# End of a top-k attention ahead of a routed expert layer: three scales and the first block of a weight split made ahead of a branch

## The chip, the cores and the metric

One core of a Trainium2 chip runs the whole kernel. The metric is the time of one execution on the device in microseconds (us). PE is TensorE, ACT is ScalarE, DVE is VectorE, POOL is GpSimd; SP issues the transfers named here.

## The reference

Attention with a top-k mask feeds a routed expert layer, whose output feeds a second layer with a rational function between its two products. Cut to what matters:

```
scores = q @ k.T / 8                       # 4 x 8 heads, 576 x 576, depth 64
mask   = scores >= 32nd largest of the row
attn   = softmax(where(mask, scores, -1e9))
x      = attn @ v                          # as (2304, 512)
logits = x @ w_gate                        # (2304, 8)
# all 2304 * 8 entries in falling order: token -> expert,
# unless the token is taken or the expert has 288 tokens
for e in range(8):
    m = assigned == e
    x2[m] = relu(x[m] @ w1[e]) @ w2[e]     # 512 x 1024, 1024 x 512
h = x2 @ w_in                              # 512 x 2048
g = (a0 + a1 h + a2 h^2 + a3 h^3) / (1 + |b0||h| + |b1|h^2 + 1e-6)
out = g @ w_out                            # 2048 x 512
```

## The kernel before

Products of the layers behind the routing run in fp16 as three products of halves: each fp32 operand is multiplied by a power of two and split into a rounded fp16 "high" and a remainder "low" (lines L1954, L1955 and L1956 are the three products). The power of two comes from a sum of squares (weights) or a maximum (x); four small DVE instructions on a 128 x 1 column turn that number into the scale and its inverse (`power_steps`, L293 to L298).

The program goes through these stages.

1. Attention, 72 units of two heads each; it ends in `finish_attention`. There a planner, the object `last` of class `Flow`, takes tasks (engine, cost, function, what they wait for, rank) and writes them out in the order in which they could start by its costs, lower ranks first; tasks of rank 1000 and above only fill. Beside the last units it places the router's logits: PE turns x (L1200), DVE copies (`xt`, L1206), PE multiplies (L1210), DVE copies (`lt`, L1221), PE turns back (L1224), DVE copies (`lg`, L1249). ACT sums x's squares there (L1228), and, as filling, the squares of the first expert's w1 and w2 (`conv_stats`, the `wsum` rows of L306).
2. A branch, `tc.If` at L1338: a value that DVE wrote (`odd`, L1305) is loaded by every engine, and where it isn't zero the attention is computed again. It is zero here, so every engine jumps over that code. Behind it the first instruction of most engines waits for all five engines' sequencers.
3. Routing: seven phases of four search steps, each a chain DVE (compare, L1552), PE (count, L1560), DVE (L1624), PE (L1628), DVE (L1636). At a phase's end PE counts with L1718. In the gaps a second planner, `flow`, places other work: the split of w_in and w_out, and the first expert's weights (`add_first`: highs on ACT, L1430; remainders on PE, L1494 twice and L1495 once for 256 columns; a copy on ACT, L1498).
4. A second branch at L1904, jumped over too. Behind it POOL gathers the first expert's rows of x (L1931, `xe`), PE turns them (L1966), ACT and DVE split them (`xT`, L1944 and L1945), and PE multiplies with w1 and w2 (`pe`). ACT and DVE take those products out (`hT`, `x`) and, between them, split what is left of w_in and w_out.
5. The second layer in pairs of product groups (`ph` from w_in, `po` from w_out), expert after expert, until the end.

The split of a weight goes in blocks of four pieces of 128 x 512 (`add_block`, called with the block's scales `s` and `inv`): w_in has four blocks (0 to 3), w_out four. Each piece arrives by a transfer on SP into a slot with its upper halves in place. ACT then makes a sign (L383), a magnitude (L384) and a shifted word (L385), or for later pieces in a ring buffer two steps (L373, L377); DVE adds the lower bits (`mantissa`, L408) and the sign (L412, or L395 for the ring), in wholes of 512 or in halves of 256 columns; ACT squares with a sum (L306, output `junk`, sum `nq`); DVE sums four sums (L427) and takes the four power steps; ACT makes the four highs (L436); DVE makes the four lows (L440), and a low frees its slot, on which SP fetches a further piece (L340). The fetches that become free behind the first branch are the eight at 463.88. A later block's highs wait for the block before to have its lows, since they write over each other's slots.

Before the first branch, the first six pieces have their three ACT steps done, and the first three of them (`EV = 3`) mantissa and sign. Everything else of `add_block` stands behind the branch, as do the first expert's two weight scales (`scale_steps`: a product with ones, L1414, a sum, L1419, four power steps) and x's scale (L1511, then `everywhere_steps`: maximum, L1391, PE turns it, L1384, maximum, L1393, PE spreads it, L1388, copy, L1395, then four power steps to `s_x` and `i_x`). x's scale is needed by `xT` and by the settling of w_in's four scales to a common one (`settle_in`, L1445 to L1447). `settle_out` does the same for w_out from `s_out` (the `ev_m` of 128 x 16).

## Time and profile before

| what | us |
|---|---|
| three runs | 1224.65, 1225.04, 1227.86 |
| median | 1225.04 |
| the profiled execution's own time | 1223.68 |
| its span, first to last instruction | 1222.0 |
| attention's last output x (DVE, L905) | 446.86 |
| the last logits' copy (DVE, L1249) | 459.45 |
| first work behind the first branch | 463.08 to 463.95 |
| the last of the routing's slots (DVE, L1798) | 560.30 |
| expert 0's products with w1, w2 begin | 574.91 |
| the first `ph` group's square sums on PE (L2086) | 620.60 |

Granted TensorE clock over the span: 0.921 of 2.4 GHz. Busy over the span: PE 91%, DVE 86%, ACT 83%, POOL 31%. These shares are means over stages with different limits: from 446 to 463 and from 463 to 560 no engine is full, from 575 to 600 PE is, from 600 to 640 ACT and DVE are, and from 700 on PE is. So a change around the routing has to be read stage by stage, and a row's idle time with its releaser (in brackets: idle before it, and what ended that) tells what the instruction came late for.

### The profile page before, as it was taken

To read this page: it belongs to the slowest core of one execution; us is meant where nothing else is said; L and a number is where in the kernel's file an instruction comes from. 1 tells how busy PE (TensorE), PEld (TensorE's weight loads), DVE (VectorE), ACT (ScalarE), POOL (GpSimd) and SP (SyncE) were. 2 spreads that over 40 slices of the span, in tenths; PEclk is the share of its full clock that TensorE was granted. 3 is DMA by queue.
4 is the path that set the end of the run, shared out by engine and by line. 5 is a ranking of instruction groups with operands and counts; after the bars stand their busy time and mean duration, and the time that the engine had idled before them with its cause. 6 is when DMAs were issued, how large, how long until landed. Compare 5 with 4: busy or idle time off the path is not lost.

```text
span 1222.0 us, 26894 instructions
## 1 busy us (share of the span) xinstructions
...
## 2 busy tenths in 40 slices
...
DMA packets 81105, 80.59 MB, mean 66 GB/s; under 512 B 59968, under 2 KB 59968, under 8 KB 80960
## 3 DMA queue, kind: packets, MB, share of 16 engines
...
q0 software_dynamic: 3072, 9.48, 2.6%
...
## 4 chain that ended last, share of the span: by engine, by line
PE 26%; issue 15%; ACT 6%; DVE 5%; POOL 1%; DMA 0%; POOLq 0%; DVEq 0%
PE pa L1954 3%; PE pa L1955 3%; PE pa L1956 3%; PE ph L1954 3%; PE ph L1955 3%; PE ph L1956 3%; PE po L1955 3%; PE po L1956 3%; PE po L1954 3%; ACT junk L306 2%; POOL out_dram L2340 1%; DVE win L440 1%; ACT w1s L1430 1%; PE pa L2329 0%; ACT wout L383 0%
## 5 line engine op out<-in xcount | busy, mean ns | idle before, releaser
L787 POOL TENSOR_TENSOR win<-sv,sg 128x576 f32<-128x576 f32 x142 | 179.1, 1282 | 64.8 <-ACT sg L782 49.2
L751 DVE MAX8 cd<-sv 128x8 f32<-128x82 f32 (+1 forms) x1008 | 178.4, 230 | 11.5 <-ACT sv L704 11.4
L1954 PE MATMUL ph<-x,win 128*128 128x288 f16 x512 | 148.8, 291 | 10.5 <-DVE uv L2223 10.5
L885 PE MATMUL po<-vm,pT 128*128 128x65 f32 (+1 forms) x1280 | 151.8, 267 | 1.6 <-issue 1.1
L1955 PE MATMUL po<-g,wout 128*128 128x288 f16 x512 | 146.7, 287 | 2.4 <-DVE g L1945 2.4
L1956 PE MATMUL ph<-x,win 128*128 128x288 f16 x512 | 148.8, 291 | 0.0
L1955 PE MATMUL ph<-x,win 128*128 128x288 f16 x512 | 148.8, 291 | 0.0
L1954 PE MATMUL po<-g,wout 128*128 128x288 f16 x512 | 146.7, 287 | 0.9 <-ACT g L1944 0.8
L1956 PE MATMUL po<-g,wout 128*128 128x288 f16 x512 | 146.7, 286 | 0.0
L885 PEld LDWEIGHTS po<-vm,pT 128*128 128x128 f32 (+1 forms) x1280 | 139.5, 182 | 4.8 <-issue 2.1
L853 PE MATMUL pt<-ident,sv 128*128 128x128 f32 x648 | 126.9, 284 | 0.3 <-ACT pT L867 0.3
...
L857 PE MATMUL pt<-dg,mk 128*128 128x128 bf16 x720 | 121.0, 222 | 1.2 <-POOL mk L844 1.2
L1931 POOL DMA_INDIRECT xe<-xrows,rows_i x24 | 24.8, 1032 | 294.6 <-PE pa L1966 272.4
L782 ACT ACTIVATE sg<-sv,cut_all 128x576 bf16<-128x576 f32 x142 | 109.0, 778 | 5.7 <-DVE cut_all L757 5.7
L2214 ACT ACTIVATE z<-ph,inv 128x288 f32<-128x288 f32 x128 | 63.8, 499 | 58.9 <-PE ph L1956 58.1
L843 ACT ACTIVATE sg<-sv,pn 128x576 bf16<-128x576 f32 x136 | 97.9, 771 | 13.2 <-POOL pn L821 13.2
L694 PE MATMUL s<-region 64*128 64x288 f32 (+1 forms) x640 | 93.3, 444 | 14.9 <-ACT region L665 10.2
L788 DVE MAX8 w<-win 128x8 f32<-128x576 f32 x142 | 105.4, 743 | 0.0
L853 PEld LDWEIGHTS pt<-ident,sv 128*128 128x128 f32 x648 | 92.9, 143 | 16.1 <-ACT sg L782 3.8
L844 POOL TENSOR_SCALAR mk<-sg 128x576 bf16<-128x576 bf16 x136 | 88.9, 672 | 1.8
L867 ACT ACTIVATE pT<-pt 128x1152 f32<-128x1152 f32 x72 | 81.5, 1132 | 4.0 <-PE pt L857 3.9
...
## 6 DMA issues: line engine op xcount, KB each, us to landing
...
```

The costliest lines, as they stand in the source:

```text
L694: nc.tensor.matmul(sc[p0 : p0 + n, 2 * hh + g, 0:w], qT[rows, j, p0 : p0 + n], kT[rows, bb, c : c + w], start=True, stop=True,)
L751: nc.vector.max(cd[:, g, :], sv[:, o : o + n])
L782: nc.scalar.activation(sg, sv_t[u, hh], AF.Sign, bias=cut_all[:, 2 * u + hh, 7:8], scale=-OVER, accum_out=t["sum"][:, c : c + 1],)
L787: nc.gpsimd.tensor_tensor(win, sv_t[u, hh], sg, op=OP.mult)
L788: later.append(lambda c=c, win=win: nc.vector.max(t["w8"][:, c, :], win))
L843: nc.scalar.activation(sg, sv, AF.Sign, bias=t["pn"][:, c : c + 1])
L853: nc.tensor.transpose(dst, pr[:, c * P : (c + 1) * P], ident)
L857: nc.tensor.matmul(dst, mk_buf[u % 2][:, o : o + P], bat[b]["dg"][:, 2 * i + hh, :], start=False, stop=True, skip_group_check=True,)
L885: nc.tensor.matmul(po[p0 : p0 + n, i, hh, :], sb[:, hh * (R + 1) + c, p0 : p0 + n], vm[:, bb, hh, c, :], start=(c == 0), stop=False,)
L1954: nc.tensor.matmul(acc, ah, bh, start=first, stop=False)
L1955: nc.tensor.matmul(acc, ah, bl, start=False, stop=False)
L1956: nc.tensor.matmul(acc, al, bh, start=False, stop=last)
```

## The change

- `EV` goes from 3 to 6: pieces 3, 4 and 5 of w_in also get mantissa and sign ahead of the branch, in wholes of 512 columns; before, these were halves in the routing's gaps.
- Block 0 of w_in (four squares, sum and power steps, four highs, four lows, and the two fetches that its lows release while pieces are left for them) is handed to `last` with rank 1004, ahead of the branch. `ins` holds blocks 1 to 3 alone, and block 1's highs no longer wait for block 0's lows.
- The first expert's two weight scales are made ahead of the branch (`first_scale_steps`, rank 1005), behind the sums of each weight.
- x's scale is made ahead of the branch (`x_scale_steps`, rank 260), and the sums of x's squares move from rank 900 to 240 so that they come earlier. `s_x` and `i_x` move to a pool that lives through the branch.
- `add_first`, `settle_in` and `add_turns` no longer wait for those scales. Where attention is computed again, x's scale is made again, and the weights' sums aren't.

The diff, cut to its core:

```diff
-    EV = 3
-
-    def add_block(i, n0, dst, s, inv, rows, rank, late, after):
+    EV = 6
+    s_x = wpool.tile([P, 1], F32, name="s_x")
+    i_x = wpool.tile([P, 1], F32, name="i_x")
+
+    def add_block(i, n0, dst, s, inv, rows, rank, late, after, ready=None, flow=flow):
...
+            if ready:
+                t = ready[n]
+            elif quick(n):
...
-                for k in range(3 if n >= 6 else 0):
+                for k in range(3 if n >= EV else 0):
...
-        lasts.append(lows)
-        return last
+        lasts.append([] if ready else lows)
+        return norms if ready else last
...
+            def first_scale_steps(which, psum):
+                st = {}
+
+                def total():
+                    st["t"] = psum()
+                    nc.tensor.matmul(st["t"], ones, w_sum.pop((which, 0)), start=True, stop=True)
+
+                def reduce():
+                    w_scale[which, 0] = [wpool.tile([P, 1], F32, name=f"w{n}{which}of0") for n in "si"]
+                    n2 = wk.tile([P, 1], F32, name=f"wnorm{which}", bufs=1)
+                    nc.vector.tensor_reduce(n2, st["t"], axis=AX.X, op=OP.add)
+                    st["steps"] = power_steps(*w_scale[which, 0], n2, 380 + 2 * (11, 13)[which - 1])
+
+                return [("P", 0.3, total), ("V", 0.15, reduce)] + [
+                    ("V", 0.15, lambda i=i: st["steps"][i]()) for i in range(4)
+                ]
+
+            def x_scale_steps(psum):
+                m = wk.tile([P, 1], F32, name="x_m", bufs=1)
+                g = wk.tile([1, 1], F32, name="x_g", bufs=1)
+                x_max = wk.tile([P, 1], F32, name="x_max", bufs=1)
+                st = {}
+
+                def turn():
+                    st["t"] = psum()
+                    nc.tensor.transpose(st["t"][0:1, 0:P], m, ident)
+
+                def spread():
+                    nc.tensor.matmul(st["t"][:, P : P + 1], ones_row, g, start=True, stop=True)
+
+                return [
+                    ("V", 0.15, lambda: nc.vector.tensor_tensor(xs, xs, xs2, op=OP.add)),
+                    ("V", 0.15, lambda: nc.vector.tensor_reduce(m, xs, axis=AX.X, op=OP.max)),
+                    ("P", 0.3, turn),
+                    ("V", 0.25, lambda: nc.vector.tensor_reduce(g, st["t"][0:1, 0:P], axis=AX.X, op=OP.max)),
+                    ("P", 0.3, spread),
+                    ("V", 0.15, lambda: nc.vector.tensor_copy(x_max, st["t"][:, P : P + 1])),
+                ] + [("V", 0.15, f) for f in power_steps(s_x, i_x, x_max, 388)]
...
-                    a = last.add("A", 0.3 if one else 0.7, norm_of, deps, 900 + t)
+                    a = last.add("A", 0.3 if one else 0.7, norm_of, deps, 240 + t)
...
+                    norms_of.append(a)
...
-                for n in range(6):
+                narrowed = {}
+                for n in range(EV):
                     t = []
                     for k in range(3):
                         t = [last.add("A", 0.55, lambda n=n, k=k: heads(n)[k][2](), t, 1000 + n)]
-                    if n < EV:
-                        t = [last.add("V", 0.6, lambda n=n: mantissa(n), t, 1000 + n)]
-                        t = [last.add("V", 0.6, lambda n=n: apply_sign(n), t, 1000 + n)]
+                    t = [last.add("V", 0.6, lambda n=n: mantissa(n), t, 1000 + n)]
+                    narrowed[n] = [last.add("V", 0.6, lambda n=n: apply_sign(n), t, 1000 + n)]
+                for f in add_block(0, 0, w_in_s, s_in, i_in, False, 1004.0, False, 1.0, narrowed, last):
+                    hold(f, "win", 3, [f])
+
+                def beside_logits():
+                    if not spares:
+                        spares.append(spare())
+                    return spares[0][:, 1, 2 * P :]
+
                 for w in (1, 2):
+                    sums_of = []
                     for c in range(4):
                         f = last.add("A", 1.04, lambda w=w, c=c: conv_stats(w, 0, c), [], 1000 + (SO if w == 1 else 3) + c)
                         hold(f, "win", 3, [f])
+                        sums_of.append(f)
+                    last.chain(first_scale_steps(w, lambda w=w: beside_logits()[:, P + 4 * w : P + 4 * w + 4]), sums_of, 1005)
+                last.chain(x_scale_steps(beside_logits), norms_of, 260)
...
                 recompute()
+                for _, _, step in x_scale_steps(lambda: spare()[:, 1, :]):
+                    step()
                 for w in (1, 2):
                     load_w(w, 0)
-                    for c in range(4):
-                        conv_stats(w, 0, c)
...
-        s_x = lpool.tile([P, 1], F32, name="s_x")
-        i_x = lpool.tile([P, 1], F32, name="i_x")
...
-            m = lpool.tile([P, 1], F32, name="ev_m", bufs=3)
-            g = lpool.tile([1, 1], F32, name="ev_g", bufs=3)
+            m = lpool.tile([P, 1], F32, name="ev_m", bufs=2)
+            g = lpool.tile([1, 1], F32, name="ev_g", bufs=2)
...
-        ins = [add_block(c, 4 * c, w_in_s, s_in, i_in, False, c - 80.0, False, 20.0) for c in range(KC)]
+        ins = [add_block(c, 4 * c, w_in_s, s_in, i_in, False, c - 80.0, False, 20.0) for c in range(1, KC)]
...
-            scaled = add_steps(scale_steps(which, 0), [], -90.0)
...
-            ), [scaled], -88.0)]
+            ), [], -88.0)]
...
-                t = flow.add("A", 0.95, lambda c=c: conv_hi(which, 0, c), [scaled], -88.0)
+                t = flow.add("A", 0.95, lambda c=c: conv_hi(which, 0, c), [], -88.0)
...
-        x_max = lpool.tile([P, 1], F32, name="x_max")
-        scaled_x = add_steps(
-            [("V", 0.1, lambda: nc.vector.tensor_tensor(xs, xs, xs2, op=OP.add))]
-            + everywhere_steps(xs, OP.max, x_max) + [("V", 0.07, f) for f in power_steps(s_x, i_x, x_max, 388)],
-            [], -85.0,
-        )
-        settled_in = add_steps(settle_in(), ins + [scaled_x], -60.0)
+        settled_in = add_steps(settle_in(), ins, -60.0)
...
-    add_turns(0, [here, scaled_x], lambda c: -200.0)
+    add_turns(0, [here], lambda c: -200.0)
```

What moves, at the three places that the prediction speaks of (line numbers of the changed kernel are some 40 to 50 higher; L442 there is L440 here, L438 is L436, L1293 is L1249, L1249 there is L1206, L2004 is L1956, L2014 is L1966, L2134 is L2086).

DVE ahead of the first branch, before: the last router copies, and then the load of the branch's value.

```order
L531 TENSOR_SCALAR span<-pt 128x1
L532 COPY span<-pt 128x1
L1206 COPY xt<-s 128x256 x2
L1221 COPY lt<-s 8x128 x2
L1249 COPY lg<-s 128x8 x2
L1338 TENSOR_LOAD odd
```

DVE at the same place in the changed kernel, from the last logits' copy on; two further power steps of w2's scale (L295, L298) and the load of the branch's value follow.

```order
L1293 COPY lg<-s 128x8
L294 TENSOR_SCALAR pw_v<-pw_e 128x1
L298 TENSOR_SCALAR wi1of_7602<-ws1of_7601 128x1
L295 TENSOR_SCALAR s_x<-pw_v 128x1
L298 TENSOR_SCALAR i_x<-s_x 128x1
L408 SCALAR_TENSOR_TENSOR win<-win 128x512
L442 SCALAR_TENSOR_TENSOR win<-win,s_in 128x512
L412 TENSOR_TENSOR win<-win 128x512
L442 SCALAR_TENSOR_TENSOR win<-win,s_in 128x512 x2
L1132 TENSOR_REDUCE wnorm_7642<-s 128x1
L293 TENSOR_SCALAR pw_e<-wnorm_7642 128x1
L294 TENSOR_SCALAR pw_v<-pw_e 128x1
```

Fourteen instructions now stand between the last logits' copy and the branch, where none stood.

ACT behind the second branch, before (`junk` is the square of a ring piece, `win<-win` and `win<-wout` are w_in's highs from slots in `win` and `wout`):

```order
L306 ACTIVATE junk,nq<-nraw_12956 128x512
L373 ACTIVATE ring_12954<-nraw_12962 128x512
L377 ACTIVATE ring_12954<-ring_12954,bias_115 128x512
L306 ACTIVATE junk,nq<-nraw_12958 128x512
L436 ACTIVATE win<-win,s_in 128x512
L1944 ACTIVATE xT_17209<-pe,s_x 128x288 x2
L436 ACTIVATE win<-win,s_in 128x512
L1944 ACTIVATE xT_17209<-pe,s_x 128x288
L436 ACTIVATE win<-wout,s_in 128x512
L1944 ACTIVATE xT_17209<-pe,s_x 128x288
L436 ACTIVATE win<-wout,s_in 128x512
```

ACT at the same place in the changed kernel:

```order
L438 ACTIVATE win<-wout,s_in 128x512 x4
L1992 ACTIVATE xT_17236<-pe,s_x 128x288
L306 ACTIVATE junk,nq<-nraw_13026 128x512
L1992 ACTIVATE xT_17236<-pe,s_x 128x288
L373 ACTIVATE ring_13022<-nraw_13032 128x512
L1992 ACTIVATE xT_17236<-pe,s_x 128x288
L438 ACTIVATE win<-wout,s_in 128x512
L1992 ACTIVATE xT_17236<-pe,s_x 128x288
L438 ACTIVATE win<-wout,s_in 128x512 x3
L306 ACTIVATE junk,nq<-nraw_13028 128x512
L377 ACTIVATE ring_13022<-ring_13022,bias_115 128x512
```

The two squares and the ring's two steps that came first now stand behind four highs of w_in (the other ring steps of this place have gone to the routing's gaps), and over the whole stretch up to the first `ph` group ACT has twelve instructions fewer: four highs of w_in, one of w_out, three squares and four ring steps.

PE ahead of the first `ph` group, before (`pe` is expert 0's last product, `ev_m` the largest of w_out's scales, `sq` the squares of expert 0's result):

```order
L1955 MATMUL pe<-hT_17261,w2s_13227 128x288
L1956 LDWEIGHTS w2s_13228
L1956 MATMUL pe<-hT_17260,w2s_13228 128x288
L1966 MATMUL pa<-ident,xe 128x96 x6
L1384 MATMUL pa<-ident,ev_m 1x128
L2086 LDWEIGHTS onesb
L2086 MATMUL pa<-sq,onesb 128x288
```

PE at the same place in the changed kernel:

```order
L2003 LDWEIGHTS w2s_13174
L2003 MATMUL pe<-hT_17284,w2s_13174 128x288
L2004 LDWEIGHTS w2s_13175
L2004 MATMUL pe<-hT_17283,w2s_13175 128x288
L2014 MATMUL pa<-ident,xe 128x96 x3
L2134 LDWEIGHTS onesb
L2134 MATMUL pa<-sq,onesb 128x288
```

The turn of `ev_m` has left the place ahead of the square sums; it stands behind the first four `ph` groups now, and three of the six turns of the next expert's x stand elsewhere.

## Rows read from the trace of the kernel before

**Rows 1.** Stretches: length; busy PE, PEld, DVE, ACT, POOL; clock; DMA; GB/s

```profile
598.00:606.00 8.00, 2.93 (x24) 2.10 (x22) 7.41 (x19) 8.00 (x16) 0.00 (x0) 0.94 0.00 1
606.00:614.00 8.00, 0.89 (x4) 0.60 (x5) 7.41 (x20) 7.87 (x20) 0.00 (x0) 0.50 0.00 0
614.00:622.00 8.00, 2.16 (x10) 1.32 (x11) 7.80 (x18) 7.97 (x17) 3.17 (x3) 0.50 0.26 74
622.00:630.00 8.00, 6.40 (x38) 4.34 (x36) 5.91 (x21) 5.28 (x9) 0.00 (x0) 0.78 0.69 262
630.00:640.00 10.00, 5.30 (x33) 3.40 (x31) 9.76 (x28) 9.73 (x19) 0.00 (x0) 0.79 0.60 205
700.00:750.00 50.00, 48.40 (x393) 38.47 (x393) 42.22 (x98) 38.77 (x73) 6.08 (x9) 1.00 0.33 109
```

**Rows 2.** Order of time around the first branch: start, length, engine, [idle before]

```profile
454.25 0.18 ACT L306 ACTIVATION_READ_ACCUMULATOR win<-region 128x1 f32 x1
...
458.74 0.28 DVE L1221 COPY lt<-s 8x128 f32<-8x128 f32 x1 [1.32 <-PE s L1224]
...
459.15 0.27 PE L1224 MATMUL s<-ident,lt 8*128 8x8 f32 x1 [0.44 <-DVE lg L1249]
459.45 0.17 DVE L1249 COPY lg<-s 128x8 f32<-128x8 f32 x1 [0.36 <-PE s L1224]
463.08 0.23 DVE L1680 COPY lc<-lg 128x144 f32<-128x144 f32 x1 [3.46 <-DVEq L1338]
...
463.85 0.21 DVE L1588 TENSOR_SCALAR rng<-span 128x1 f32<-128x1 f32 x1 [0.48 <-PEq L1338]
...
463.91 0.66 ACT L306 ACTIVATE junk<-win 128x512 bf16<-128x512 f32 x1 [9.48 <-PEq L1338]
```

**Rows 3.** Order of time in the routing's first and last phase

```profile
467.48 0.83 DVE L1552 TENSOR_TENSOR cmp<-vt,thr 128x288 bf16<-128x288 f32 x2
...
469.52 0.83 DVE L1552 TENSOR_TENSOR cmp<-vt,thr 128x288 bf16<-128x288 f32 x2
...
542.56 0.83 DVE L1552 TENSOR_TENSOR cmp<-vt,thr 128x288 bf16<-128x288 f32 x2
...
545.12 0.83 DVE L1552 TENSOR_TENSOR cmp<-vt,thr 128x288 bf16<-128x288 f32 x2
...
549.58 0.67 PE L1718 MATMUL pt<-asel,onesb 128*128 128x8 bf16 x18
```

**Rows 4.** Order of time behind the second branch

```profile
566.00 0.16 DVE L1395 COPY x_max<-pa 128x1 f32<-128x1 f32 x1 [5.55 <-PE pa L1388]
...
573.69 0.93 DVE L1945 SCALAR_TENSOR_TENSOR xT<-pe,s_x,xT 128x288 f16<-128x288 f32 x2
...
574.91 0.45 PE L1954 MATMUL pe<-xT,w1s 128*128 128x288 f16 x1
...
612.90 0.74 PE L1966 MATMUL pa<-ident,xe 96*128 96x96 f32 x3 [11.97 <-DVE xT L1945]
...
614.48 2.71 ACT L436 ACTIVATE wout<-wout,s_out 128x512 f16<-128x512 f32 x4
...
615.78 2.73 DVE L440 SCALAR_TENSOR_TENSOR wout<-wout,s_out 128x512 f16<-128x512 f32 x4
...
620.43 0.37 PE L1384 MATMUL pa<-ident,ev_m 128*1 128x128 f32 x1 [5.84 <-DVE ev_m L1391]
```

**Rows 5.** Groups, 463 to 660 us: count, busy us, mean ns

```profile
L306 ACT ACTIVATE junk<-win 128x512 bf16<-128x512 f32 x6 | 3.9, 657 | 9.7 <-PEq L1338 9.5 <-DVE win L412 0.2
L373 ACT ACTIVATE ring<-nraw 128x512 bf16<-128x512 bf16 x4 | 3.1, 768 | 0.0
L408 DVE SCALAR_TENSOR_TENSOR nraw<-nraw,ring 128x256 uint32<-128x256 uint32 x8 | 3.2, 414 | 0.0
L408 DVE SCALAR_TENSOR_TENSOR region<-region 128x512 uint32<-128x512 uint32 x8 | 5.5, 682 | 0.0
L294 DVE TENSOR_SCALAR pw_v<-pw_e 128x1 int32<-128x1 uint32 x9 | 1.3, 147 | 0.0
```

2 lines of the change are left out of this document (1 added, 1 removed).

## The prediction

> **What bounds the kernel now.** I read the stretches first, because no engine bounds the whole span. From 700 us on PE is busy 48.40 of 50 [rows 1]: what comes before is paid in full there, since PE then works through the pairs without gaps. Between 598 and 640 it is the other way round: ACT is busy 8.00, 7.87 and 7.97 of 8 in the first three stretches, DVE 7.41, 7.41 and 7.80, and PE stands idle for 5.07 + 7.11 + 5.84 + 1.60 + 4.70 = 24.3 us over the five [rows 1]. PE's two long waits there are both for DVE: 11.97 us for `xT` at 612.90 and 5.84 for `ev_m` at 620.43 [rows 4]. So work that leaves ACT's and DVE's queues between 566 and 640 moves the end. The second view is the order of time around the first branch. ACT is done at 454.43 and then idle for 9.48; DVE's last logits' copy ends at 459.62, PE's last turn at 459.42 [rows 2]. DVE's first instruction behind the branch comes 3.46 after its last, at 463.08, and then waits 0.48 for PE's sequencer, until 463.85, which is 4.43 after PE's last [rows 2]. So that stretch is paced by DVE's and PE's chain, and DVE has 0.48 of slack against PE. I call 463.85 the join: every engine's first work that needs the others begins there. The routing is a chain of short steps: 2.04 us a step without a product of `add_first` on PE (467.48 to 469.52), 2.56 with one (542.56 to 545.12) [rows 3].
>
> **Ahead of the first branch: a cost.** ACT gets four squares and four highs more. By duration that is 4 x (0.66 + 0.18 for reading the sum) + 4 x 0.68 = 6.1 us [rows 2, 4, 5], behind an end at 454.43, so 460.5 at most, and about 459.5 since one sign moves into an earlier gap. Behind it stand PE's product with ones (about 0.3, as the turn of 0.27 [rows 2]), a sum on DVE and four dependent power steps at some 0.2 each: 461 to 462.
>
> DVE gets more. Fourteen instructions stand between the last logits' copy and the branch (the order above): nine small ones at 0.147 [rows 5], one mantissa and one sign at 0.68 [rows 5], and three lows at 2.73 / 4 = 0.68 [rows 4], together 1.3 + 1.4 + 2.05 = 4.7 us. Nothing hides these; before, the copy was DVE's last. Where the copy itself comes is less clear. About fourteen small instructions and one low are set between the router's copies (2.7 us), and four short products between PE's; much of it fits into waits of that chain (1.32, 0.36, 0.44 near its end [rows 2]), and the last-but-one tile no longer waits behind the last one's product. Followed in order with these durations the copy ends at 458.6; I allow 457.7 to 461.6. DVE then ends at 463.3. With the 3.46 of the branch, and 0.29 for what it did between 463.08 and the wait, the join moves from 463.85 to about 467.0. **Cost: +3.1, bounds +0.6 (ACT's chain alone, 460.7) and +6.2.** PE (done by 460) and SP (two issues, as soon as two lows are made) come earlier than DVE; ACT's own price for the branch is not seen, and it would have to be over 7 us to decide.
>
> **Routing: a small gain.** Of DVE's filling twelve halves go and nine others come, and some twelve small ones vanish; they stood in the search's gaps, so I put them at nothing, and where a gap was too short for them it is a gain. The products can start in the first phase, as the scales are ready. That makes its steps 2.56 instead of about 2.27 (three steps, +0.9), takes one product out of a later step (-0.5), and frees the end: the count at 549.58 has products of the last phase ahead of it, which are done before that phase then; I take -0.7 there [rows 3], and as much again because the products are through earlier and no late copy of ACT holds one back. **Together -1.0, bounds -2.5 and +1.0** (above zero if the products of phase one also delay its end).
>
> **Behind the second branch: the gain.** Until the first `ph` group ACT has five highs at 0.68, three squares at 0.84 and four ring steps at about 0.77 fewer: 3.4 + 2.5 + 3.1 = 9.0, of which neighbours overlap by some 0.05 each, so 8.5; one square and one high come back later (-1.5), which leaves 7.0 [rows 2, 4, 5]. DVE has nine halves at 0.41, four lows at 0.68 and some eighteen small ones fewer: 3.7 + 2.7 + 2.6 = 9.0, with 2.4 coming back: 6.6 [rows 4, 5]. The start of expert 0's products moves little: DVE has 7.4 us of work ahead of its first `xT` low, where it has 7.7 now (566.00 to 573.69 [rows 4]), because the lows of the next block take the places that x's scale and block 0 leave. The products then hold PE from 574.91 [rows 4] to about 600.9 (2.93 of the stretch from 598 [rows 1]), whatever the others do. The gain falls behind them, where ACT and DVE are full and PE waits. The wait of 5.84 for `ev_m` goes as such (its turn stands behind four `ph` groups), and what is late next is `xT` and the square sums, which ACT's and DVE's queues reach about 7 us sooner. That later half of the stretch also holds idle time of both engines, 2.7 on ACT and 2.1 on DVE in 622 to 630 [rows 1], while `ph` was late; part of it is used when `ph` is earlier. Against that, ACT can run dry beside the products. **I take -6.9, the ACT work; bounds -4 (3 us of it lost in waiting for products and gathered rows) and -12** (`ph` starting near 609 with nothing late after it).
>
> Sum: +3.1 - 1.0 - 6.9 = -4.8. The profiled run took 1223.68 (1222.0 of span and 1.68 around it), so it would take 1218.9; the median lies 1.36 above that run, so I predict 1225.04 - 4.8 = **1220.2**.
>
> **The rivals.**
> *The tail takes the gain back (slower).* One mechanism: DVE's end ahead of the branch. If the small steps and lows between the router's copies lengthen the chain instead of filling its waits, the copy comes 2 to 3.7 later, and the join 6.2 to 7.9 later. From a tail of 6.9 + 1.0 = 7.9 on the kernel is slower at my middle gain; at the gain's lower bound of 4 and an even routing, from 4.0 on. With 7.9 against 4.0: +3.9, 1228.9. For it: DVE is in order and every added low stands in line with router copies. Against it: DVE waits 1.32 for PE at 458.74 and 0.36 at 459.45 [rows 2], so part of the work has room.
> *The work is moved, not gained (same).* The stretch behind the branch gives only its lower bound, since PE's products up to 600.9 fix the stage, and the tail costs its 3.1: -0.9, 1224.1. For it: DVE's work ahead of the first `xT` hardly falls. Against it: the 24.3 us of idle PE behind the products.
> *The gain converts more than once (much faster).* Freed of the wait for `ev_m`, `ph` starts 12 us sooner and nothing is late after it: +3.1 - 1.0 - 12 = -9.9, 1215.1. Against it: ACT and DVE still owe the rest of w_out's splits to the first `po` groups.
> On the clock the trace shows 0.50 of full speed, so 1.2 GHz, from 606 to 622, while PE had the two waits, and 0.78 and 0.79 on average up to 640 [rows 1]. The Trainium skill (TensorE: Matmul & The Clock Gate, HAM oscillation) says that an array left idle falls to half clock and pays that again for every burst behind a wait. By that rule `ph` groups that start sooner, straight behind a wait, would still run at 1.2 GHz at first, which speaks for the middle forecast over this rival; if the waits closed altogether, the 6.40 + 5.30 us of PE at about 0.785 would shrink by 2.5, and the rival would give 1212.6.
>
> **How the numbers follow.** Chances: forecast 0.52 (1216.5 to 1223.5 is its own range), moved 0.20, slower 0.17, much faster 0.11. A measurement can tell about 0.3% (3.7 us) from no change, so faster means below 1221.3: nearly three quarters of the forecast's case (0.38) and the much faster one (0.11), 0.49. Slower, above 1228.7, is most of the slower case, 0.14. The rest, 0.37, is the same. The range goes from 1214.5, past the middle of the much faster case, to 1228.5, just short of the slower one, and leaves out about 0.18.
>
> **What would show it.** Right: DVE's last instruction ahead of the branch near 463 and the join near 467; the routing's seven phases about 1 us shorter in sum; behind the second branch the first `ph` group 8 us or more sooner, counted from the second branch, and PE's idle time between 600 and 640 down by 6 to 8. Wrong: a join later than 470; a last logits' copy later than 461; ACT idle beside the products by as much as was taken from it; or waits of PE beyond 640 that were not there, for lows and highs of w_out.

## The result and the profile after

The changed kernel takes 1231.62 us (median of 8 runs, 1230.92 to 1235.55) against 1225.17 for the kernel before on the same chip: ratio 1.0063, interval 1.0051 to 1.0076. By the medians it is slower by 6.45 us, and the time lies above the predicted range. Its profiled execution has a span of 1229.4 us at a granted clock of 0.924 (before 1222.0 at 0.921).

Three stretches add up to the difference. "Last x" is attention's last output on DVE (L905 before, L909 after), "join" is `rng` (L1588, now L1636), "slots" is the last of the routing's slots (L1798, now L1846), and the routing is counted from its first `top` to the slots.

| us | before | after | difference | predicted |
|---|---|---|---|---|
| last x | 446.86 | 446.98 | | |
| last x to the last logits' copy | 12.59 | 15.80 | +3.2 | -1.0 |
| copy to DVE's last work | 0.17 | 4.63 | +4.5 | +4.7 |
| DVE's last work to its first behind the branch | 3.46 | 5.50 | +2.0 | 0 |
| its first work there to the join | 0.77 | 0.51 | -0.3 | -0.5 |
| last x to the join | 16.99 | 26.44 | +9.45 | +3.1 |
| routing | 95.99 | 98.60 | +2.6 | -1.0 |
| slots to the first `ph` group | 61.26 | 52.07 | -9.2 | -8 or more |
| slots to the end of the span | 661.70 | 656.93 | -4.8 | -6.9 |

The first stretch of the changed kernel, in order of time (start, length, engine; in brackets the idle time before it and what ended it). These rows answer to [rows 2].

```profile
459.04 1.02 PE L1253 MATMUL s<-xt,wg 128*8 128x128 f32 x4 [0.26 <-DVE lg L1293]
...
460.10 0.28 DVE L1156 TENSOR_REDUCE x_g<-s 1x1 f32<-1x128 f32 x1 [0.98 <-PE s L1253]
...
460.50 1.02 PE L1253 MATMUL s<-xt,wg 128*8 128x128 f32 x4 [0.44 <-DVE wnorm L1132]
...
462.07 0.28 DVE L1264 COPY lt<-s 8x128 f32<-8x128 f32 x1 [0.78 <-PE s L1150]
...
462.78 0.17 DVE L1293 COPY lg<-s 128x8 f32<-128x8 f32 x1
...
465.18 1.41 DVE L442 SCALAR_TENSOR_TENSOR win<-win,s_in 128x512 f16<-128x512 f32 x2
...
465.95 1.00 SPq L340 DMA_DIRECT2D win<-in_moe_w_in_dram  x2
...
467.26 0.15 DVE L298 TENSOR_SCALAR wi2of<-ws2of 128x1 int32<-128x1 int32 x1
472.62 0.40 ACT L1540 ACTIVATE diag<-ident,ws1of 128x128 f32<-128x128 f32 x1 [10.83 <-DVEq L1395]
...
472.83 1.59 POOL L1425 MEMSET ring<- 128x512 uint32 x3 [54.88 <-SPq L1395]
472.91 0.53 DVE L1728 COPY lc<-lg 128x144 f32<-128x144 f32 x1 [5.50 <-DVEq L1395]
...
473.42 0.20 DVE L1636 TENSOR_SCALAR rng<-span 128x1 f32<-128x1 f32 x1
```

The router's last products and the scales' products write the same PSUM tile, `s`. DVE's reading of x's maxima (460.10) waits 0.98 for the router's products, PE's next router products (460.50) wait for DVE's sum of the first weight, and the router's copy `lt` (462.07) ends its wait at a scale's product, L1150. None of the 14 instructions from 462.86 to 467.41 waits for another engine; they take 4.46 us from the copy's end. Then DVE idles for 5.50.

The second stretch: DVE's and ACT's rows in the routing, which answer to [rows 3].

```profile
527.24 0.83 DVE L1600 TENSOR_TENSOR cmp<-vt,thr 128x288 bf16<-128x288 f32 x2
...
529.15 1.35 ACT L383 ACTIVATE region<-region 128x512 int8<-128x512 bf16 x1
530.53 1.33 ACT L384 ACTIVATE region<-region 128x512 bf16<-128x512 bf16 x1
...
532.61 0.64 ACT L306 ACTIVATE junk<-wout 128x512 bf16<-128x512 f32 x1
...
533.37 0.16 DVE L429 TENSOR_REDUCE nq<-nq 128x1 f32<-128x4 f32 x1 [4.90 <-ACT junk L306]
...
534.54 0.83 DVE L1600 TENSOR_TENSOR cmp<-vt,thr 128x288 bf16<-128x288 f32 x2
```

One search step takes 7.30 us, from 527.24 to 534.54, where its like takes 2.56 [rows 3]. DVE's sum of the squares of block 2 of w_in (533.37) stands in line ahead of the search and waits 4.90 us for a square that ACT reaches behind its work on raw pieces. By that one wait the routing comes out longer: the first phase takes 1.2 us more than before (11.30 against 10.11), this step 4.7 more, and everything else together is 3.3 shorter.

The third stretch, behind the second branch: stretches (columns as in [rows 1]), and two waits of PE, of which the first answers to that of 11.97 in [rows 4] and the second is new.

```profile
640.50:649.50 9.00, 6.09 (x48) 4.51 (x46) 8.65 (x30) 8.97 (x18) 0.00 (x0) 1.00 0.01 3
649.50:658.50 9.00, 6.20 (x48) 4.68 (x48) 9.00 (x15) 9.00 (x15) 0.00 (x0) 1.00 0.30 82
658.50:667.50 9.00, 7.05 (x36) 4.62 (x36) 6.81 (x11) 6.85 (x14) 0.00 (x0) 0.62 0.59 196
```

```profile
617.84 0.47 PE L2014 MATMUL pa<-ident,xe 96*128 96x96 f32 x3 [3.83 <-DVE xT L1993]
...
660.45 0.40 PE L2002 MATMUL ph<-x,win 128*128 128x288 f16 x1 [4.31 <-DVE uv L2271]
```

The wait of 11.97 has shrunk to 3.83, that of 5.84 for `ev_m` is gone, and `ph` starts 9.2 us sooner. But PE then idles 2.9, 2.8 and 2.0 us in three stretches with ACT and DVE full in the first two, has a new wait of 4.31, and the granted clock is 0.62 on average in the third stretch; from 659 to 666 it is 0.51, so about 1.2 GHz. The last block of w_out's splits, whose highs came 60 to 69 us behind the slots before, now comes at 71 to 79.

Counted from the slots, the two kernels' stretches up to 80 us and from 80 to 140 us behind them are these, first before, then after:

```profile
560.30:640.00 79.70, 44.16 (x295) 32.22 (x296) 68.61 (x181) 68.92 (x130) 9.71 (x9) 0.74 0.34 115
640.00:700.00 60.00, 55.57 (x439) 43.25 (x438) 53.08 (x105) 56.68 (x101) 0.00 (x0) 0.98 0.21 72
```

```profile
572.47:652.17 79.70, 52.44 (x352) 38.09 (x353) 67.91 (x171) 65.75 (x125) 9.78 (x9) 0.84 0.24 77
652.17:712.17 60.00, 52.32 (x403) 40.14 (x400) 49.82 (x95) 52.91 (x93) 0.00 (x0) 0.94 0.40 141
```

PE's idle time falls from 35.5 to 27.3 us in the first and rises from 4.4 to 7.7 in the second: 8.3 gained, 3.2 given back.

### The profile page after: what moved, and what is told of

Same layout as the page of the kernel before. It is cut to its first block, busy times and chain, and to the rows that moved or that the text cites. A ratio compares the mean times of both kernels' runs of the same rounds, so it can differ in the third digit from the quotient of the medians.

```text
span 1229.4 us, 26890 instructions
## 1 busy us (share of the span) xinstructions
PE 1113.9 (91%) x9717; PEld 900.3 (73%) x9717; DVE 1055.8 (86%) x4087; ACT 1022.6 (83%) x1816; POOL 381.2 (31%) x488
## 4 chain that ended last, share of the span: by engine, by line
PE 25%; issue 15%; DVE 7%; ACT 4%; DMA 1%; POOL 1%; POOLq 0%; DVEq 0%
PE pa L2002 3%; PE pa L2004 3%; PE pa L2003 3%; PE po L2002 3%; PE po L2003 3%; PE po L2004 3%; PE ph L2002 3%; PE ph L2004 3%; PE ph L2003 3%; ACT junk L306 1%; POOL out_dram L2388 1%; DMA region<-in_moe_w_dram 1%; DVE wout L442 1%; DVE uv L2271 1%; DVE w2s L1490 0%
## 5 line engine op out<-in xcount | busy, mean ns | idle before, releaser
L2004 PE MATMUL ph<-x,win 128*128 128x288 f16 x512 | 147.9, 289 | 0.0
L2004 PE MATMUL po<-g,wout 128*128 128x288 f16 x512 | 146.9, 287 | 0.0
L698 PE MATMUL s<-region 64*128 64x288 f32 (+1 forms) x640 | 95.8, 453 | 14.6 <-ACT region L669 9.6
L708 ACT ACTIVATE sv<-s 128x1152 f32<-128x1152 f32 x72 | 80.6, 1120 | 4.8 <-PE s L698 2.4
```

The costliest lines, as they stand in the source:

```text
L698: nc.tensor.matmul(sc[p0 : p0 + n, 2 * hh + g, 0:w], qT[rows, j, p0 : p0 + n], kT[rows, bb, c : c + w], start=True, stop=True,)
L2004: nc.tensor.matmul(acc, al, bh, start=False, stop=last)
```

## The experiments

Theory: the tail ahead of the first branch costs more than its instructions, by a shared tile and by the branch itself, and the plan behind it wastes part of the gain. Rival: the work moved ahead of the branch is worth less behind it than I thought. Each run's stretches are read from one profiled execution, the ratio (to the kernel before, same chip) from several runs. Last x lies between 445.6 and 450.4 in these executions, with the low clock in different places ahead of it (granted clock from 430 to 446 us: 1.00 after, 0.79 in e7_lows_last, where last x is at 450.4); so the tail is counted from last x. Where that comes at 450, the stretch to the copy is about 1 us shorter (14.75 in e9_costs, 15.80 after, by the same instructions).

How far one execution can be trusted differs by column. Five kernels with the same order in the routing (after, e1_own, e2_late, e7_lows_last, e12_rank) have it at 98.58 to 98.68. But before and e14_before_costs, which have the same instructions ahead of the branch, take 12.59 and 13.28 to the copy; and after and e1_own, which have the same order on every engine behind the branch, take 656.93 and 659.12 from the slots to the end, as e9_costs and e15_own_order_costs do with 649.55 and 651.55. So a difference under some 2 us in that column can be one of executions.

| us | x to copy | DVE idle at branch | x to join | routing | slots to end | ratio (interval) |
|---|---|---|---|---|---|---|
| before | 12.59 | 3.46 | 16.99 | 95.99 | 661.70 | |
| after | 15.80 | 5.50 | 26.44 | 98.60 | 656.93 | 1.0063 (1.0051 to 1.0076) |
| e1_own | 13.49 | 5.33 | 23.94 | 98.67 | 659.12 | 1.0054 (1.0038 to 1.0071) |
| e2_late | 15.59 | 3.84 | 24.49 | 98.68 | 656.67 | 1.0066 (1.0044 to 1.0088) |
| e3_scales | 16.16 | 3.88 | 21.24 | 97.26 | 658.92 | 1.0035 (1.0023 to 1.0046) |
| e4_block | 13.47 | 1.15 | 18.45 | 95.50 | 657.29 | 0.9975 (0.9963 to 0.9987) |
| e5_ev6 | 14.07 | 3.29 | 18.22 | 97.16 | 662.09 | 1.0004 (0.9986 to 1.0022) |
| e6_block_late | 13.37 | 1.06 | 18.27 | 94.24 | 659.03 | 0.9982 (0.9966 to 0.9998) |
| e7_lows_last | 12.26 | 2.83 | 20.61 | 98.61 | 657.11 | 1.0018 (1.0003 to 1.0032) |
| e8_nq | 15.58 | 5.45 | 26.12 | 96.80 | 656.32 | 1.0037 (1.0021 to 1.0052) |
| e9_costs | 14.75 | 5.68 | 25.53 | 93.96 | 649.55 | 0.9982 (0.9966 to 0.9998) |
| e10_all | 13.44 | 2.55 | 21.76 | 96.70 | 659.38 | 1.0012 (0.9995 to 1.0030) |
| e12_rank | 15.41 | 5.64 | 26.25 | 98.58 | 657.44 | 1.0051 (1.0031 to 1.0070) |
| e13_block_rank | 13.36 | 1.09 | 18.28 | 95.68 | 657.67 | 0.9995 (0.9979 to 1.0012) |
| e14_before_costs | 13.28 | 3.46 | 17.40 | 95.13 | 657.61 | 0.9966 (0.9953 to 0.9979) |
| e11_block_costs | 13.16 | 1.34 | 18.32 | 95.75 | 651.40 | 0.9939 (0.9921 to 0.9958) |
| e15_own_order_costs | 12.26 | 2.78 | 20.56 | 93.95 | 651.55 | 0.9941 (0.9922 to 0.9960) |
| e16_all_costs | 13.31 | 2.75 | 21.83 | 93.94 | 650.78 | 0.9941 (0.9921 to 0.9961) |

### One part at a time: e1_own, e2_late, e3_scales, e4_block

e1_own gives the scales a PSUM tile of their own, one of attention's output tiles; so in the plan they also wait for attention's averaged outputs (the list `averaged`):

```diff
+                own = []
                 def beside_logits():
-                    if not spares:
-                        spares.append(spare())
-                    return spares[0][:, 1, 2 * P :]
+                    if not own:
+                        own.append(ps_o.tile([P, 512], F32, name="po"))
+                    return own[0][:, 0 : 2 * P]
```

> The changed kernel with the three scales' PE results in a PSUM bank of their own (the one of the attention's outputs, free by then) instead of in the tile that holds the router's last logits; the order of all instructions ahead of the first branch stays the same. In the changed kernel the last logits' copy starts at 462.78 and the first DVE work behind the branch at 472.91. Theory 'shared tile': the scales' reads and writes stand in line with the last tiles' products, because each waits for the other's use of the tile, so without it the last copy comes 2 to 3 us sooner (459.8 to 460.8), the join too, and the time is 1228.6 to 1229.6 against 1231.6. Rival 'DVE's own queue': it is the number of instructions on DVE that delays the copy, which stays within 0.5 us of 462.78, and the time within 1 us of 1231.6.

e2_late holds the two transfers that block 0's lows start until behind the branch:

```diff
-            fetch(raw_t.pop(n0 + g))
+            (held.append if ready else fetch)(raw_t.pop(n0 + g))
...
+        for slot in held:
+            fetch(slot)
```

> The changed kernel with the two fetches that block 0's lows release issued behind the branch instead of ahead of it (behind the eight others, on SP); everything else ahead of the branch stands in the same order. In the changed kernel DVE's first work behind the branch comes 5.50 after its last ahead of it, before 3.46. Theory 'transfers': the two transfers under way lengthen the branch (its loads and code come by transfers too), so the wait falls to 3.4 to 3.8 and the time by 1.5 to 2.2, to about 1229.7. Rival 'place of the branch in the code' : the wait stays at 5.3 to 5.6 and the time within 1 us of 1231.6.

e3_scales makes the scales alone ahead of the branch (three mantissas, no block 0), and e4_block the six mantissas and block 0 alone:

```diff
-    EV = 6
+    EV = 3
...
-                for f in add_block(0, 0, w_in_s, s_in, i_in, False, 1004.0, False, 1.0, narrowed, last):
-                    hold(f, "win", 3, [f])
```

> Only the three scales are made ahead of the branch; pieces 3 to 5 and block 0 stay where they were before the change. Theory 'sum of three causes': the last logits' copy is late by 2 to 3 (shared tile), four power steps stand behind it (0.8), no transfers are under way: join at 467 to 468 against 463.85 before and 473.42 after. Behind the second branch the gain is that of x's scale alone, 1 to 2. Time 1226 to 1229. Rival 'the block makes the delay': join within 1 us of 463.85 and a time of 1223 to 1225.

```diff
-                    last.chain(first_scale_steps(w, lambda w=w: beside_logits()[:, P + 4 * w : P + 4 * w + 4]), sums_of, 1005)
-                last.chain(x_scale_steps(beside_logits), norms_of, 260)
```

> Only pieces 3 to 5 and block 0 of w_in are made ahead of the branch; the three scales stay where they were before the change. Theory 'sum of three causes': the last logits' copy comes within 1 us of 459.45, 3.4 us of mantissa, sign and lows stand behind it, and the two transfers lengthen the branch by 2: join at 469 to 470. Behind the second branch most of the gain is there, 3.5 to 4.5 of 4.8. Time 1226 to 1229 if the routing is as before, up to 4.7 more if DVE waits for a late square in it. Rival 'the scales make the delay': join at 466 or sooner and a time of 1221 to 1224.

The shared tile costs 2.3 us: the copy comes 13.49 behind last x in e1_own, 15.80 after. The other runs agree: with the shared tile 15.41 to 15.59 (e2_late, e8_nq, e12_rank), with its own 13.31 and 13.44 (e16_all_costs, e10_all), and where last x is at 450, 14.75 against 12.26. The expected time of 1228.6 to 1229.6 did not come: the median is 1230.79, and a ratio of 1.0054 can't be told from 1.0063. The rival, DVE's own queue, falls. In e3_scales, without block 0, the copy is as late as after, and the same pattern stands in its rows (DVE, then the copy):

```profile
459.55 0.16 DVE L1132 TENSOR_REDUCE wnorm<-s 128x1 f32<-128x4 f32 x1 [1.21 <-PE s L1243]
...
466.50 0.15 DVE L1293 COPY lg<-s 128x8 f32<-128x8 f32 x1
```

So the scales make the tail long, and e3_scales came within its expected 1226 to 1229 (1227.57). They are not the whole loss: scales alone give 1.0035 and block 0 alone 0.9975, which together would be 1.0010, and the changed kernel has 1.0063. More than half of what it lost is there only with both. The table shows where: the join is 4.25 later with the scales, 1.46 with the block, 9.45 with both; the routing +1.3, -0.5 and +2.6. e4_block is faster than both kernels, against the expected 1226 to 1229; its rival ("the scales make the delay") named the join (465.65) rightly, and the median of 1220.85 is just under its range. In its execution nearly the whole gain behind the slots is there (-4.4 of -4.8).

e2_late shows what the transfers do: without them the branch costs DVE 3.84 us instead of 5.50. Whether that shortens the whole its four runs don't tell: they lie between 1228.26 and 1233.95, ratio 1.0066 with an interval down to 1.0044. e4_block has the same transfers, and there DVE idles 1.15 only:

```profile
462.00 0.67 DVE L412 TENSOR_TENSOR win<-win 128x512 f32<-128x512 f32 x1
462.61 1.40 DVE L440 SCALAR_TENSOR_TENSOR win<-win,s_in 128x512 f16<-128x512 f32 x2
465.16 0.23 DVE L1684 COPY lc<-lg 128x144 f32<-128x144 f32 x1 [1.15 <-DVEq L1342]
```

The records of DVE's sequencer explain it. The trace has the branch instruction, which stands with the sequencer and not with the engine, and the next one that the sequencer comes to. It also has the fetches of instructions: between those two there is one of 8192 bytes in each of these kernels (two in after and e1_own, 0.2 apart at most). I take it for DVE's own, by its place:

```
                       before   e2_late  e3_scales  after    e1_own   e4_block
DVE's last work ends   459.62   466.44   467.28     467.41   465.43   464.00
branch instruction     460.09   466.92   467.75     467.89   465.91   462.09
fetch begins           461.13   467.96   468.79     470.21   468.27   463.14
sequencer goes on      462.98   469.81   470.69     472.44   470.30   465.05
first work behind      463.08   470.28   471.15     472.91   470.77   465.16
branch to fetch          1.04     1.04     1.04       2.32     2.36     1.06
branch to going on       2.89     2.90     2.93       4.55     4.39     2.96
```

The branch itself takes 2.9 us where the two transfers are held back, absent, or issued only behind the branch instruction (463.37 in e4_block), and 4.4 to 4.6 where they were issued ahead of it. Of that difference 1.3 us lie ahead of the fetch, which begins 1.04 us behind the branch instruction, and with the transfers 2.3. Their packets fill the DMA engines after from 466.0 to 470.5 (share 0.74) and no longer (0.02):

```profile
466.00:470.50 4.50, 0.00 (x0) 0.00 (x0) 1.27 (x6) 0.00 (x0) 0.00 (x0) 0.50 0.74 239
470.50:473.00 2.50, 0.00 (x0) 0.00 (x0) 0.09 (x1) 0.38 (x2) 0.17 (x1) 0.50 0.02 5
```

That the transfers make the fetch later is shown by e2_late, which differs in them alone; that it stands in line behind their packets is not shown, as it begins 0.5 us (after) and 1.1 us (e1_own) before the last of them ends.

The Trainium skill (Runtime: NRT & Kernel Launch, Instruction fetch mechanics) says that a taken branch whose target isn't near makes the engine fetch the target by DMA before it goes on. The trace agrees: DVE's sequencer goes on 1.85 us behind the start of a fetch before, and 2.23 after.

The second part is where the branch instruction stands. Before and after it comes some 0.5 us behind the end of DVE's work, so nothing covers it: after, the last five instructions are the second weight's scale, each of which waits for the one before. In e4_block it comes 1.92 us ahead of that end, for the sequencer had gone on to the branch while two lows that wait for nothing were still to run.

### Is it the order, the transfers, the sum? e5_ev6 to e8_nq

e5_ev6 is the kernel before with six mantissas:

```diff
-    EV = 3
+    EV = 6
```

> The kernel before with one number changed: six raw pieces' mantissas and signs instead of three are made ahead of the first branch; block 0 and the scales stay behind it. It tells how much of e4_block's 3.2 us is the mantissas' and how much block 0's. Theory (block 0 gives it, since its squares, highs and lows are ACT and DVE work behind the second branch): time within 1.2 us of the kernel before, 1223 to 1225, with 3 mantissas and 3 signs (4.1 us) ahead of the branch, of which those that wait for nothing lie beside the branch, so that the join comes at 464 to 465.5; from the count of routed rows to the end of the span 660 to 662 (before 661.70). Rival (the mantissas alone take DVE's halves out of the routing's gaps and of the stretch behind it): 1221 or less, and count to end under 659.

Ratio 1.0004 and 662.09 from the slots to the end: the mantissas alone give nothing, and e4_block's gain is block 0's.

e6_block_late is e4_block with the edit of e2_late.

> e4_block with the two transfers that block 0's lows start held back until behind the branch. In e4_block SP passes the branch at about 470.1, 5.8 us behind its last issue, and DVE's ev_m in the search then waits 1.48 us for it. Theory (SP stands at the branch until its transfers have landed, and the search pays for it): SP passes near 464, the 1.48 is gone, the routing from its first top to the count takes 93.8 to 94.4 (95.50 in e4_block), and the time is 1.0 to 1.8 below e4_block's, near 1219.4. Rival (the wait only takes the place of a later one, or the transfers are missed later): routing shorter, but count to end longer by as much, time within 0.5 of e4_block's 1220.85. The join itself stays at 465.3 to 466 by both.

The expected chain of causes was there: SP is past the branch when it issues at 463.68, where e4_block's SP comes at 470.50, the wait of 1.48 is gone, and the routing is 94.24. But the time did not fall (0.9982 against 0.9975), as the rival said. A gain of 1 us would not show in these intervals, and the 1.7 by which slots to end is longer is within what two executions differ by.

e7_lows_last is e1_own with block 0's last two lows behind the second weight's scale:

```diff
-            t = flow.add("V", 0.66, lambda g=g: low(g), [t], rank + LOWS + 0.1, late)
+            t = flow.add("V", 0.66, lambda g=g: low(g), [t] + (list(gate) if g >= 2 else []), rank + LOWS + 0.1, late)
...
-                    last.chain(first_scale_steps(w, lambda w=w: beside_logits()[:, P + 4 * w : P + 4 * w + 4]), sums_of + averaged, 1005)
+                    ends = [last.chain(first_scale_steps(w, lambda w=w: beside_logits()[:, P + 4 * w : P + 4 * w + 4]), sums_of + averaged, 270)]
+                for f in add_block(0, 0, w_in_s, s_in, i_in, False, 1004.0, False, 1.0, narrowed, last, ends):
```

> e1_own (the changed kernel with a PSUM tile of its own for the scales) with DVE's last seven instructions ahead of the branch in another order: the scale of the second weight first (sum and four dependent power steps), the block's last two lows, which wait for nothing that is late, behind it. Same work, same two transfers. Theory (DVE's sequencer goes to the branch when the last instruction with an open wait is released, and work that waits for nothing lies beside the branch): DVE's last work still ends near 465.4, but its first work behind the branch comes near 467.5 to 468.5 instead of 470.77, 2 to 3.2 us sooner, and the span falls by about as much, to 1226.5 to 1227.5. Rival (every engine waits until SP, whose transfers are issued last, has passed the branch): SP's last issue is then near 465.5 to 466, its passing 5.5 to 5.9 behind it at 471 to 472, and DVE's first work no sooner than that: span no shorter than e1_own's 1229.5.

```profile
466.52 0.15 DVE L298 TENSOR_SCALAR wi2of<-ws2of 128x1 int32<-128x1 int32 x1
466.59 1.41 DVE L442 SCALAR_TENSOR_TENSOR win<-win,s_in 128x512 f16<-128x512 f32 x2
...
467.36 1.00 SPq L340 DMA_DIRECT2D win<-in_moe_w_in_dram  x2
470.53 0.40 ACT L1544 ACTIVATE diag<-ident,ws1of 128x128 f32<-128x128 f32 x1 [7.18 <-DVEq L1399]
...
470.82 0.23 DVE L1732 COPY lc<-lg 128x144 f32<-128x144 f32 x1 [2.83 <-DVEq L1399]
...
473.98 2.19 ACT L1489 ACTIVATE w1s<-region,ws1of 128x1024 f16<-128x1024 f32 x2 [3.05 <-SPq L1399]
```

By reordering alone DVE's idle time falls from 5.33 to 2.83 and the join comes 3.3 sooner behind last x, 1.2 of it by the shorter stretch to the copy where x is late. Both parts of the branch have shrunk: its instruction, at 467.15, now comes 0.84 ahead of the end of DVE's work instead of 0.48 behind it, and takes 3.20 instead of 4.39, since the transfers are issued behind it (467.36). SP is not past the branch until 473.98, 3.2 behind DVE: the join does not wait for SP, and that rival falls. So DVE's and ACT's first work behind the branch (470.82, 470.53) does not wait for all five sequencers, though the section on the kernel before says so of most engines. Ratio 1.0018, against 1.0054 for e1_own.

e8_nq tells the planner that the sum of block 2 is ready 3 us later:

```diff
-        scaled = flow.chain(steps[:-1], norms, rank, late)
+        slow = [("N", 3.0, lambda: None)] if i == 2 and not rows else []
+        scaled = flow.chain(slow + steps[:-1], norms, rank, late)
```

> The changed kernel with one planner entry: 3 us of delay, without an instruction, between the squares of block 2 of w_in and DVE's sum of them, so that the sum is set two steps later in the search. In the changed kernel that sum stands in line ahead of the search and waits 4.90 us for ACT, which is behind three region pieces. Theory (this one wait is all of the routing's loss): the wait falls under 1, the routing takes 93.5 to 94.5 from first top to count (98.60 in the changed kernel), and the span falls by 3 to 4.7, to 1224.7 to 1226.4, since the rest behind the count starts from the same work. Rival (ACT is the bound of that stretch, and something else of the search or of the products waits for it instead): routing 96.5 or more, span within 1.5 of 1229.4.

The 4.90 is gone, but the routing falls by 1.8 only (ratio 1.0037). PE's and DVE's rows show the next in line:

```profile
531.33 1.22 PE L1549 MATMUL pl<-region,diag 128*128 128x256 f32 x2 [2.64 <-ACT w2s L1553]
...
533.57 0.16 DVE L1673 TENSOR_SCALAR_CACHE_REDUCE over<-pl 32x8 bf16<-32x8 f32 x1 [3.33 <-PE pl L1609]
```

A product of `add_first` waits 2.64 for ACT's copy of an earlier one, and the search behind it 3.33 for PE. ACT itself is late there, so both theories were half right.

### Why ACT is late: e9_costs, e10_all, e12_rank, e13_block_rank

A raw piece has three steps on ACT, L383 to L385. The planner counts 0.52, 0.52 and 0.61 us for them. ACT's groups in the routing (count, busy us, mean ns), first of the changed kernel from 474 to 573 us, then of the kernel before from 464 to 560, show 1.35, 1.36 and 0.75, so 3.4 to 3.5 us for a piece that the plan takes for 1.65:

```profile
L384 ACT ACTIVATE region<-region 128x512 bf16<-128x512 bf16 x8 | 10.6, 1361 | 0.1
L383 ACT ACTIVATE region<-region 128x512 int8<-128x512 bf16 x8 | 10.5, 1354 | 0.0
L385 ACT ACTIVATE region<-region,bias 128x512 uint32<-128x512 uint16 x8 | 5.8, 745 | 0.1
```

```profile
L383 ACT ACTIVATE region<-region 128x512 int8<-128x512 bf16 x8 | 10.5, 1342 | 0.0
L384 ACT ACTIVATE region<-region 128x512 bf16<-128x512 bf16 x7 | 9.3, 1333 | 0.1
L385 ACT ACTIVATE region<-region,bias 128x512 uint32<-128x512 uint16 x6 | 4.5, 750 | 0.1
```

e9_costs is the changed kernel with these costs:

```diff
-                    t = [flow.add("A", (0.52, 0.52, 0.61)[k], lambda n=n, k=k: heads(n)[k][2](), t, rank + 0.5, late)]
+                    t = [flow.add("A", (1.35, 1.35, 0.75)[k], lambda n=n, k=k: heads(n)[k][2](), t, rank + 0.5, late)]
```

> The changed kernel with one entry of the planner's costs set to what the trace shows: the three ACT steps of a region piece at 1.35, 1.35 and 0.75 us instead of 0.52, 0.52 and 0.61. Theory (the routing's loss comes from ACT being fuller between 516 and 534 than the planner counts, so that the sum of block 2 and, when that is moved, the copies of the second weight's products stand behind region pieces): the planner spreads the pieces, no DVE wait over 2 us for ACT is left in the search, and the routing from its first top to the count takes 94 to 96.5 (98.60 in the changed kernel, 96.80 when only the sum was moved). Rival (ACT simply has too much work in the routing now): the wait shrinks by no more than 2, routing over 97.5, or the routing gains and count to end rises from 656.9 by as much, since the region pieces come later.

The routing falls to 93.96, and slots to end to 649.55, which I had not expected: ratio 0.9982. The sum of block 2 comes without a wait, and behind the slots PE is busier in the stretches that answer to those of after (DVE's row, then stretches, columns as above; the last from 80 to 140 us behind the slots):

```profile
532.92 0.15 DVE L429 TENSOR_REDUCE nq<-nq 128x1 f32<-128x4 f32 x1
```

```profile
638.00:647.00 9.00, 7.05 (x55) 5.39 (x55) 7.98 (x22) 8.97 (x19) 0.00 (x0) 1.00 0.29 110
647.00:656.00 9.00, 7.46 (x57) 5.27 (x56) 8.22 (x13) 9.00 (x17) 0.00 (x0) 1.00 0.00 0
656.00:665.00 9.00, 8.52 (x72) 6.71 (x70) 8.82 (x22) 8.69 (x17) 0.00 (x0) 1.00 0.61 220
649.85:709.85 60.00, 55.92 (x457) 44.20 (x456) 51.61 (x101) 53.61 (x97) 0.10 (x1) 1.00 0.30 106
```

From 80 to 140 us behind the slots PE idles 4.1 us, where it idled 7.7 after: what the changed kernel gave back there is gone.

e10_all has the edits of e1_own, e2_late, e7_lows_last and e8_nq together, without e9_costs' entry.

> The changed kernel with the four causes taken away together: a PSUM tile of its own for the scales, the block's last two lows last ahead of the branch, its transfers held until behind the branch, the sum of block 2 two steps later. Theory (these four are the whole of what was missed ahead of the count): from attention's last x to the join 19.5 to 20.8 us (16.99 before, 26.44 in the changed kernel), routing 96.3 to 97.3 (95.99 before), count to end 656 to 657.5 (661.70 before): the sum is -4 to +0.5 against the kernel before, 1220.5 to 1225. Rival (what one takes away the next wait takes back): join or routing over these numbers, span above 1224, no faster than 1226.

Routing as expected, join 1 us later than expected (which was taken from e7_lows_last, with its late last x), slots to end 659.38, over the expected 657.5: 1.0012. These four are not the whole.

e12_rank and e13_block_rank give the last block of w_out rank 1 instead of 6, in the changed kernel and in e4_block:

```diff
-        RL = [float(v) for v in "-2 1 3 6".split()]
+        RL = [float(v) for v in "-2 1 3 1".split()]
```

> The changed kernel with one rank changed: the last block of w_out's splits gets rank 1 instead of 6. In the changed kernel its highs come 71 to 79 us behind the count of routed rows, in the kernel before 60 to 69, though every other block comes sooner; the pairs' steps and the next expert's squares, which are ready sooner, go ahead of it. Then ph waits 4.31 us for DVE at 660.45, and the clock stands at half from 86.7 to 93.5 us behind the count. Theory (that late block gives back what the early start of ph gained): highs at 62 to 71, the 4.31 shrinks under 2, count to end falls from 656.9 to 653 to 655.5. Rival (ACT and DVE are full there, so whatever goes first, PE waits the same): count to end within 1 of 656.9, with the wait at another place. Ahead of the count nothing changes.

> e4_block (six mantissas and block 0 ahead of the branch, scales left behind it) with the same rank for the last block of w_out's splits, 1 instead of 6. Theory as for e12_rank: count to end from 657.3 to 653.5 to 656, span 1215 to 1217.6, ratio to the kernel before 0.994 to 0.997. Rival (full engines): count to end within 1 of 657.3 and ratio as e4_block's, 0.9975.

The block's highs come 61 to 65 us behind the slots, and nothing is gained (657.44, 657.67). The wait of 4.31 shrinks to 2.55 in e12_rank, and others come up, such as one of 4.98 at 631.01 in e13_block_rank. That this block was late is not the cause; the rival held. e13_block_rank's ratio, 0.9995, is even above e4_block's, with intervals that overlap.

### Whose gain is the entry's? e14_before_costs, e11_block_costs, e15_own_order_costs, e16_all_costs

The kernel before, e4_block, and the changed kernel with the edits of e7_lows_last (which holds e1_own's) and then e2_late's too, all with e9_costs' entry.

> The kernel before with the same cost entry as e9_costs (region pieces at 1.35, 1.35, 0.75). Theory A (the loss comes from the change and the wrong entry together, since the wait of the search for ACT is there only with the scales made ahead): routing 95 to 96.5 (95.99 before), count to end 658 to 662 (661.70), time within 0.3% of the kernel before, 1220 to 1226. Theory B (the entry helps every version alike behind the count, since the late blocks of w_out are better placed): count to end falls by 5 to 8, time 1215 to 1218, ratio 0.992 to 0.995, and the change on top of it is slower again by 0.3 to 0.6%.

> e4_block with the same cost entry. Theory A (with the right entry the early work converts, as in e9_costs): count to end from 657.3 to 650 to 653, join as in e4_block at 464 to 466, routing 94 to 96: span 1210 to 1214.5, ratio 0.990 to 0.995, the fastest of all. Theory B (the gain of the entry in e9_costs came from the scales' place in the plan): count to end 655 to 658, ratio near 0.997.

> The changed kernel with the cost entry, the scales in a PSUM tile of their own, and the block's last two lows last ahead of the branch. Theory (the tail's loss and the plan's loss add up): from attention's last x to the join 20 to 21 (25.5 in e9_costs, 20.61 in e7_lows_last), routing 93.5 to 95, count to end 649 to 652: 4 to 5 below e9_costs relative to the same chip's kernel before, ratio 0.993 to 0.996. Rival (what starts sooner waits later): the join moves by 5, the end by 2 or less, ratio 0.997 or more.

> e15 with the two transfers held until behind the branch. By e6_block_late and e10_all holding them gives a shorter branch (1 to 2 us) and takes 1.5 to 2.5 back behind the count. Theory (the transfers' place is worth nothing on balance): join 19.5 to 20.5 behind the last x, ratio within 0.15% of e15's. Rival (with the right plan the later arrival is covered): 1 to 2 us below e15.

The entry helps the kernel before as well, by 0.34% (slots to end 657.61), between the two theories. e11_block_costs came out by its theory A, e15_own_order_costs in all its numbers. Against that better kernel the change as written is not faster (0.9982 against 0.9966, intervals overlap), block 0 alone comes out 0.27% below it (0.9939), and the whole change with its tail mended 0.25% (0.9941 twice). These intervals overlap at their ends, so the 0.25% between them is likely, not sure. e11_block_costs, e15_own_order_costs and e16_all_costs are the fastest of the study, at medians of 1215.46 to 1216.49 us, and can't be told apart. Holding the transfers gained no time that shows in any of three pairs (e2_late, e6_block_late, e16_all_costs). e16_all_costs' join, expected at 19.5 to 20.5, came at 21.83, again since that number was taken from executions with a late last x.

## Why the prediction was wrong, point by point

**"Followed in order with these durations the copy ends at 458.6"** failed. The durations were right, but I let the small steps fill waits as if they met the router's steps on DVE only. They share the tile `s`, so PE's and DVE's accesses to it take turns, and the copy ended at 462.95, beyond the 461.6 that I allowed. A tile of their own gives 2.3 us of the 4.2 back (e1_own); the rest is the gain of 1.0 that did not come, and 0.9, hardly more than the 0.7 by which two executions of the same instructions differ.

**"With the 3.46 of the branch"** failed. I carried it as a constant. It is 5.50 after, 3.84 without transfers in flight (e2_late), 2.83 with two free lows at the end (e7_lows_last) and 1.15 where no scale stands there (e4_block). Both of its drivers were in the change: the order ends with five dependent steps, so that the branch instruction comes behind DVE's work, and the lows issue two transfers ahead of it, which make the branch itself 1.65 us longer (4.55 against 2.90).

**The 4.7 us of instructions behind the copy** was right: 4.46. ACT was done at 461.79, over the "460.5 at most", which decided nothing. The lower bound of the join, "ACT's chain alone, 460.7", does not fit the 461 to 462 that the same passage gives for that chain; by those it is +0.9 to +1.9.

**"Together -1.0"** for the routing failed, +2.6. What I priced came near: the first phase cost 1.2, where I had 0.9, and the rest gave 3.3, where I had 1.9. The failed step is a wait that was not in the sum, 4.7 us in one search step: I priced the products and DVE's gaps, and did not ask whether ACT could keep up with the order. The trace of before already had a raw piece's steps at 1.34, 1.33 and 0.75 us, against 0.52, 0.52 and 0.61 in the plan. With the entry mended the routing goes from 95.13 to 93.95 (e14_before_costs to e15_own_order_costs): -1.2.

**"I take -6.9, the ACT work; bounds -4"**: the sign and `ph` 9.2 sooner were right, the size was -4.8, inside the bounds. PE's idle time fell by 8.3 up to 80 us behind the slots, and 3.2 came back as waits by 140, one of the signs of being wrong that I had named. With the entry mended it is -6.1 (657.61 to 651.55) and -8.1 in e9_costs, two executions of one order.

**The rivals.** "The tail takes the gain back" came true in its place and more than in its price: I gave the join 6.2 to 7.9, it was 9.45, because the 2.0 of the branch was not in it. Its own sum, 1228.9, was still 2.7 short: it took the routing as even, which cost 2.6, and the gain behind the slots as 4, which was 4.8. My 0.17 was too little, for the argument against it looked at room on DVE and not at who else waits on the tile. "Moved, not gained" describes the end after `ph`, in part. On the clock, the first `ph` groups did run low: behind PE's wait of 3.83 up to 617.84 the granted clock was 0.72 from 618 to 624 and 0.63 from 624 to 628, where `ph` begins, then 0.94 and 1.00. Of the other signs of being wrong two came: a join later than 470 (473.42) and a copy later than 461 (462.78).

**The whole.** Mending the tail takes 0.45% off the changed kernel (1.0063 to 1.0018, e7_lows_last), the cost entry 0.81% (0.9982, e9_costs), both 1.22% (0.9941, e15_own_order_costs), so the two about add up; 0.34% of it the entry gives the kernel before too. Against that better kernel the three terms are then +3.2 for the join (17.40 to 20.56; +4.4 in e16_all_costs, without the late last x), -1.2 for the routing and -6.1 (-6.8) behind the slots: -4.1 and -3.6, where I had summed +3.1, -1.0 and -6.9 to -4.8. The medians differ by 2.7 and 3.8. So the sum came near for the work that the change moves, partly by luck: in the join the copy came no sooner (13.28 and 13.31 behind last x, where I had -1.0), and the branch was 0.7 cheaper than the 3.46 that I had carried. What made the kernel slower are three things that come with where the work was put: a shared tile, an uncovered branch, and a plan that counts ACT short.

**Still open.** Which part of e9_costs' new order shortens slots to end by 7.4 is not separated; the place of w_out's last block is not it (e12_rank). The plan also counts the two steps of a ring piece (L373, L377) at 0.52 each, where they take 0.76 and 0.87 on average in the changed kernel's routing (474 to 573 us); no run mends that. That the 8192-byte fetch is DVE's rests on its place in time, behind DVE's branch instruction.
